# First keys from ScalarE's queue, first queries pooled by VectorE, and new due times in an attention and expert kernel

## The chip, the cores and the metric

The kernel runs on one core of one Trainium2 chip. The metric is the device time of one execution in microseconds. Times of single steps come from one profiled execution, counted from the start of its span.

## What is computed

```python
q_pool = q.reshape(B, H, S // 2, 2, D).mean(axis=3)      # 2, 8, 576, 64
scores = q_pool @ k.T / sqrt(D)                           # 576 x 1152 for each head
attn = softmax(scores);  x = attn @ v                     # heads side by side: 1152 x 512
p = domain_probs / domain_probs.sum(-1)
x = sum over 4 experts: p[:, e] * (relu(x @ w1[e]) @ w2[e])
out = (silu(x @ w_gate) * (x @ w_val)) @ w_out            # 1152 x 512
```

All in float32 to the outside, with S = 1152, D = 64. Inside, operands of most products are split into a high and a low half (`hi`, `lo`) that are multiplied separately.

## The kernel before

The attention is cut into 32 units. A unit is one head and half of its pooled queries (288 of them); 16 units make a batch element. A unit is computed transposed: nine chunks of 128 keys each give a score tile of 128 keys x 288 queries (`score`, two matmuls for each chunk: the query's high and low half). ScalarE copies the scores of two chunks at a time out of PSUM (`copy_scores`, L566), VectorE takes the running maximum over chunks (`max_scores`, acc, L577; L573 and L574 for the ninth). TensorE transposes the maximum (`turn_max`, mt, L583), VectorE reduces it (top, L593), TensorE spreads it over the partitions (m, L605). VectorE and POOL subtract it (L622), ScalarE takes the exponential (L628), TensorE multiplies with the values (av, L655), and ScalarE and VectorE take numerator and denominator (num, den). In the second batch element the exponentials are split as well (eh on ScalarE, el on VectorE or POOL, L640).

Keys and queries come in raw and are turned by TensorE. Keys of two heads are loaded together (`load_k`); a key tile is turned in three groups of three chunks (`prep_k`, L492) into PSUM and split per head: the high half by ScalarE (kt, L508), the low half by VectorE (L510). Queries of two units are loaded together (`load_q`, L475) and pooled: POOL adds each two neighbours and copies the sum beside itself (`prep_pool`, L484 and L485). TensorE turns them (`prep_q`, L518), ScalarE takes the high half (qhi, L529) and VectorE the low one (qlo, L534). The names in the rows of the order are these tiles: kraw and qraw raw keys and queries, tr their transposes in PSUM, kt, qhi and qlo the split operands, s a unit's scores, sc scores in PSUM.

The work of the experts fills TensorE between the units: `experts` multiplies the first batch element's rows with the first weights. Eight hidden tiles of the first expert get the first half of their sum early (part); later the other half follows, VectorE adds the early part (L996), ScalarE takes the high half with the relu (hhi) and VectorE the low half (hlo, L1005).

What order all this stands in is set by `Plan`: each step is given a due time, an engine, a cost and what it reads, writes and takes (buffers, PSUM banks). `Plan.arrange` replays the steps with these costs, each engine taking the ready step of the lowest due time, and the program is written in that order. The due times come from the table `DUE`, one value for each kind of step and phase: units 0 to 7, 8 to 15, 16 to 31. The numbers `E0_START`, `E00_START`, their rates and the `SPLIT` pairs place the experts' products and weight splits. The chip then runs each engine's row strictly in order.

At the start everything is due at once: SP's queue issues two query transfers, six key transfers (three groups, two heads), then the values. The first three key groups and the two query transposes use the PSUM banks c and d.

Of the kernel before, what the change touches and what calls it, by code (L numbers as in the profile page):

```python
# [8 lines left out]
F32 = mybir.dt.float32  # L9
# [20 lines left out]
    "mt": (4.55, -10.52, 4.08),  # L30
    "top": (15.12, 6.72, 2.47),
    "mb": (0, 7.53, 0.71),
    "mcopy": (4.54, 5.02, 2.02),
    "sub0": (5.37, 5.37, 6.98),
    "sub1": (10.75, 19.17, 24.25),
    "sub2": (18.85, 13.58, 25.88),
    "exp0": (25.25, 26.41, 12.68),
    "exp1": (26.62, 16.94, 14.5),
    "exp2": (15.82, 20.58, 17.57),
    "hi0": (14.41, 14.41, 24.01),  # L40
    "hi1": (16.21, 16.21, 16.21),
    "hi2": (16.25, 16.25, 16.25),
    "lo0": (13.1, 13.1, 13.1),
    "lo1": (15, 15, 15),
    "lo2": (17.1, 17.1, 17.1),
    "av": (18.94, 17.93, 11.82),
    "finish": (-54.35, -171.81, -27.68),
    "inv0": (0.7, 0.7, 0.7),
    "inv1": (2.54, 2.54, 2.54),
    "scale": (2.4, 2.4, 2.4),  # L50
    "xhi": (3.2, 3.2, 3.2),
    "xlo": (3.7, 3.7, 3.7),
    "copy": (-0.74, -7.74, -2.17),
    "max": (0.25, 0.25, -12.78),
    "q0": (-9.93, 3.24, 2.94),
    "q1": (3.52, 4.53, -1.14),
    "qhalf": (0.4, -0.01, -3.27),
    "k0": (-7.53, -3.37, -11.67),
    "k1": (-1.07, 0.04, -2.03),
    "k2": (6.33, 3.09, 6.04),  # L60
    "v": (6.7, 6.7, 9.56),
    "khalf": (-0.27, -0.27, -0.27),
}
SPLIT = (0.43, 4.71)
EARLY_SPLIT = (4.47, 10.35)
E0_START = 162.2
E0_RATE = 9.292
E00_START = 95.52
E00_RATE = 1.625
# [164 lines left out]
def tile_kernel(  # L234
# [14 lines left out]
    P = 128  # L249
# [168 lines left out]
    def load_k(jj, n=KC):  # L418
        b, j = divmod(jj, NPAIR)
        kr = raw.tile([P, KC, 2, D], F32, tag="kraw", name=f"kraw{jj}")  # L420
        for c in range(0, KC, n):
            for i in range(2):
                src = k[b, 2 * j + i].rearrange("(p c) d -> p c d", c=KC)
                nc.sync.dma_start(out=kr[:, c : c + n, i, :], in_=src[:, c : c + n])
        kraws[jj] = kr
# [54 lines left out]
    def prep_pool(g):  # L480
        qr = qps[g] = qraws.pop(g)
        rows = qr.rearrange("p a b d -> p (a b) d")
        first, second = rows[:, :, 0:D], rows[:, :, D : 2 * D]
        nc.gpsimd.tensor_tensor(out=first, in0=first, in1=second, op=ALU.add)  # L484
        nc.gpsimd.tensor_copy(out=second, in_=first)  # L485
# [209 lines left out]
    def plan_attention():  # L695
        def during(u):
            phase = 2 if u >= UPB else u // (UPB // 2)
            return {name: times[phase] for name, times in DUE.items()}
# [6 lines left out]
        def due_k(jj, g, t, bank):  # L705
# [4 lines left out]
            for i in range(2):  # L710
                at(
# [25 lines left out]
        def due_load_k(jj, t, n=KC):  # L737
            parts = [("kr", jj, g) for g in range(3)]
            at(t, "SP", 1.0, load_k, jj, n, writes=parts, takes=[("kraw", ("kraw", jj))])

        def due_load_q(g, t):
            tag = "acc" if g == 1 else "qraw"
            at(t, "SP", 0.9, load_q, g, writes=[("qr", g)], takes=[(tag, ("qr", g))])
# [4 lines left out]
        def due_pool_q(g, t):  # L748
            at(t, "POOL", 1.5, prep_pool, g, writes=[("qr", g)], kind="port")

        start = -20
        due_load_q(0, start)
        due_load_k(0, start, 3)
# [7 lines left out]
        due_k(0, 0, start, "d")  # L761
        due_k(0, 1, start + 1, "d")
        due_k(0, 2, start + 1, "c")
        due_q(1, start + 2, "d")
# [1153 lines left out]
```

## Time and profile before

| | us |
|---|---|
| median of 3 runs | 884.59 (883.41 to 884.64) |
| profiled execution, its own time | 884.53 |
| span of the profiled execution | 882.8 |
| TensorE (PE) busy | 860.8 |
| VectorE (DVE) busy | 648.8 |
| ScalarE (ACT) busy | 518.5 |
| POOL busy | 449.7 |

The span runs from the first to the last instruction; 1.7 us lie around it. A busy time counts an engine's instructions with the tail of each, so a busy TensorE may still start its matmuls further apart than it could. What an engine waits for is read from its rows: the number in brackets behind an instruction is the idle time before it and the step that ended it.

### The profile page before, as it was taken

What the parts mean: (1) busy time and instruction counts of PE and PEld (TensorE: products, weight loads), DVE (VectorE), ACT (ScalarE), POOL (GpSimd) and SP (SyncE); (2) the same over time, 40 slices, a digit from 0 to 9 for tenths busy, and PEclk for the clock granted to TensorE, in tenths of its full rate; (3) what the DMA queues carried; (4) which work ended last, traced back from release to release, by engine and by line L of the source; (5) the groups of instructions that cost most, each with busy time, mean ns of one, the idle gap of its engine ahead of it and who ended that gap; (6) DMA issues with size and microseconds to landing.
All of it is one profiled execution on the core that took longest, in us unless ns stands there. A gap on an engine that the chain in (4) does not pass through costs nothing.

```text
span 882.8 us, 14130 instructions
## 1 busy us (share of the span) xinstructions
PE 860.8 (98%) x5292; PEld 789.4 (89%) x5292; DVE 648.8 (73%) x956; ACT 518.5 (59%) x887; POOL 449.7 (51%) x326
## 2 busy tenths in 40 slices
PE   5999999989999999999999999999999999999998
PEld 4788888778888889888899999999999999998886
DVE  5788888897667777656587778987659977886550
ACT  5888888886787777767343342343335455555422
POOL 3666764976777987978423324533011444336000
PEclk9999999999999999999999999999999999999999
DMA  6112232132323322221357788887451122221202
GB/s 147 42 41 76 55 90 62 56 96 79 101 63 87 98 68 69 61 72 48 109 172 246 249 246 255 268 267 226 147 167 36 43 86 83 94 92 34 99 25 108
DMA packets 131317, 98.48 MB, mean 112 GB/s; under 512 B 33328, under 2 KB 118320, under 8 KB 131248
## 3 DMA queue, kind: packets, MB, share of 16 engines
q1 hardware_dynamic: 131248, 97.57, 36.7%
q8 instruction: 42, 0.69, 0.3%
q14 instruction: 27, 0.22, 0.1%
HBM read 82.07 MB, written 15.48 MB: 111 GB/s over the span
## 4 chain that ended last, share of the span: by engine, by line
PE 90%; DVE 4%; ACT 4%; issue 1%; DMA 0%; POOL 0%; SPq 0%; DVEq 0%; ACTq 0%; POOLq 0%
PE ps L938 45%; PE P L938 14%; PE av L655 12%; PE out L938 8%; PE sc L548 4%; PE sc L549 4%; ACT s L566 1%; PE mt L583 1%; ACT s L628 1%; DVE acc L577 1%; PE m L605 1%; PE tr L492 1%; PE tr L518 1%; DVE kt L510 0%; ACT kt L508 0%
## 5 line engine op out<-in xcount | busy, mean ns | idle before, releaser
L372 ACT ACTIVATE whi<-wraw 128x512 fp32r<-128x512 f32 x128 | 80.7, 630 | 136.5 <-PE ps L938 111.9
L622 POOL TENSOR_TENSOR s<-s,m 128x864 f32<-128x864 f32 x64 | 134.0, 2112 | 47.0 <-ACT m L615 46.1
L938 PE MATMUL ps<-xhi,whi 128*128 128x320 f32 (+1 forms) x384 | 131.4, 342 | 1.0 <-DVE hlo L1005 0.9
L938 PE MATMUL ps<-hhi,whi 128*128 128x320 f32 (+1 forms) x384 | 130.4, 339 | 0.2 <-DVE hlo L1005 0.2
L938 PE MATMUL ps<-hhi,wlo 128*128 128x320 f32 (+1 forms) x384 | 129.3, 337 | 0.1
L938 PE MATMUL ps<-xhi,wlo 128*128 128x320 f32 (+1 forms) x384 | 129.3, 337 | 0.0
L938 PE MATMUL ps<-xlo,whi 128*128 128x320 f32 (+1 forms) x384 | 129.2, 336 | 0.0
L938 PE MATMUL ps<-hlo,whi 128*128 128x320 f32 (+1 forms) x384 | 129.2, 336 | 0.0
L378 DVE TENSOR_TENSOR wlo<-wraw,whi 128x512 fp32r<-128x512 f32 x96 | 84.9, 884 | 40.9 <-ACT whi L372 39.8
L566 ACT ACTIVATE s<-sc 128x576 f32<-128x576 f32 (+1 forms) x160 | 93.5, 599 | 20.8 <-PE sc L549 18.9
L628 ACT ACTIVATE s<-s 128x864 f32<-128x864 f32 x96 | 87.9, 922 | 15.5 <-DVE s L622 12.4
L548 PE MATMUL sc<-qhi,kt 128*128 128x288 f32 x288 | 93.2, 340 | 3.8 <-DVE acc L577 3.6
L549 PE MATMUL sc<-qlo,kt 128*128 128x288 f32 x288 | 81.4, 298 | 0.0
L938 PE MATMUL P<-opT,wq 128*128 128x288 f32 x576 | 81.0, 296 | 0.4 <-ACT s L1388 0.3
L938 PEld LDWEIGHTS P<-opT,wq 128*128 128x128 f32 x576 | 78.1, 188 | 0.9 <-ACT s L1388 0.6
L655 PE MATMUL av<-s,v 128*128 128x288 f32 x288 | 78.6, 411 | 0.0
L938 PEld LDWEIGHTS ps<-hhi,wlo 128*128 128x128 f32 x384 | 72.1, 188 | 5.7 <-DVE wlo L378 0.4
L938 PEld LDWEIGHTS ps<-xhi,wlo 128*128 128x128 f32 x384 | 72.1, 188 | 5.5
L938 PEld LDWEIGHTS ps<-xhi,whi 128*128 128x128 f32 x384 | 72.1, 188 | 4.8 <-DVE hlo L1005 1.7
L1042 POOL TENSOR_TENSOR yacc<-yacc,yt 128x512 f32<-128x512 f32 (+2 forms) x32 | 39.4, 1243 | 71.9 <-DVE yt L1021 66.5
L938 PEld LDWEIGHTS ps<-hhi,whi 128*128 128x128 f32 x384 | 72.1, 188 | 4.3 <-DVE hlo L1005 0.5
L938 PEld LDWEIGHTS ps<-hlo,whi 128*128 128x128 f32 x384 | 72.1, 188 | 3.9
(120 smaller groups left out, 2014.1 us busy)
## 6 DMA issues: line engine op xcount, KB each, us to landing
wraw<-in_moe_w_dram SPq DMA_DIRECT2D x128, 256.0 KB, 2.9
w<-in_moe_w_gate_dram SPq DMA_DIRECT2D x12, 512.0 KB, 5.1
w<-in_moe_w_val_dram SPq DMA_DIRECT2D x12, 512.0 KB, 5.1
wd<-wk SPq DMA_DIRECT2D x12, 512.0 KB, 3.1
w<-in_moe_w_out_dram SPq DMA_DIRECT2D x12, 512.0 KB, 4.3
wr<-wd SPq DMA_DIRECT2D x12, 512.0 KB, 4.1
qraw<-in_q_dram SPq DMA_DIRECT2D x32, 144.0 KB, 2.5
wd<-ws SPq DMA_DIRECT2D x12, 384.0 KB, 4.9
```

Source lines behind the costliest of these rows:

```text
L372: nc.scalar.activation(out=hi, in_=t, func=AF.Copy)
L378: eng.tensor_tensor(out=lo, in0=t, in1=hi.bitcast(F32), op=ALU.subtract)
L492: nc.tensor.matmul(pt[:, m * P : (m + 1) * P], kr[:, c].rearrange("p h d -> p (h d)"), ident, is_transpose=True,)
L518: nc.tensor.matmul(pt[:, t * QT : (t + 1) * QT], qp[:, i, t, :], ident[:QT, :QT], is_transpose=True,)
L548: nc.tensor.matmul(ps, wt, qhi, start=True, stop=False)
L549: nc.tensor.matmul(ps, wt, qlo, start=False, stop=True)
L566: nc.scalar.activation(out=s[:, c : c + n, :], in_=ps[:, :n, :W], func=AF.Copy)
L622: eng.tensor_tensor(out=sg, in0=sg, in1=m.unsqueeze(1).to_broadcast([P, 3, W]), op=ALU.subtract)
L628: nc.scalar.activation(out=sg, in_=sg, func=AF.Exp)
L655: nc.tensor.matmul(avs[u][:, :W], w[:, c].rearrange("p t d -> p (t d)"), e, start=(c == 0 and n == 0), stop=(c == KC - 1 and n == len(term ...
L938: nc.tensor.matmul(ps, w, x, start=first and n == 0, stop=last and n == len(terms) - 1)
L1042: eng.tensor_tensor(out=y, in0=y, in1=t, op=ALU.add)
```

## The change

Four things. (1) `load_k` can load a part of a key tile, and the parts ahead of the last go out from ScalarE's queue: the first head pair's first two key groups are issued by ScalarE, ahead of its table load, and the third by SP behind the queries. (2) `prep_pool` of the first query tile runs on VectorE, the others stay on POOL. (3) The first keys' transposes use banks e, f and d, and each group's split of the second head gets a due time of its own (`START_I0` to `START_I2`); the groups and the second query get due times of their own as well. (4) Units 0 to 2 are a phase of their own with a fourth column in `DUE`, and some 25 values of the other columns and of the experts' placement are changed. No step is added or dropped otherwise.

```diff
 DUE = {
-    "top": (15.12, 6.72, 2.47),
+    "top": (6.99, 6.72, 2.47, 9.2),
-    "sub1": (10.75, 19.17, 24.25),
+    "sub1": (7.26, 19.17, 23.94, 10),
...
-E0_START = 162.2
-E0_RATE = 9.292
-E00_START = 95.52
-E00_RATE = 1.625
+E0_START = 163.36
+E0_RATE = 9.454
+E00_START = 93.4
+E00_RATE = 1.465
+START_I0 = 4.6
+START_I1 = 6.6
+START_I2 = 8.6
+START_K1 = 0.5
+START_K2 = 1.0
+START_Q1 = -0.04
...
-    def load_k(jj, n=KC):
+    def load_k(jj, n=KC, first=0, last=KC):
         b, j = divmod(jj, NPAIR)
-        kr = raw.tile([P, KC, 2, D], F32, tag="kraw", name=f"kraw{jj}")
-        for c in range(0, KC, n):
+        if jj not in kraws:
+            kraws[jj] = raw.tile([P, KC, 2, D], F32, tag="kraw", name=f"kraw{jj}")
+        kr = kraws[jj]
+        eng = nc.sync if first or last == KC else nc.scalar
+        for c in range(first, last, n):
             for i in range(2):
                 src = k[b, 2 * j + i].rearrange("(p c) d -> p c d", c=KC)
-                nc.sync.dma_start(out=kr[:, c : c + n, i, :], in_=src[:, c : c + n])
-        kraws[jj] = kr
+                eng.dma_start(out=kr[:, c : c + n, i, :], in_=src[:, c : c + n])
...
-        nc.gpsimd.tensor_tensor(out=first, in0=first, in1=second, op=ALU.add)
-        nc.gpsimd.tensor_copy(out=second, in_=first)
+        eng = nc.gpsimd if g else nc.vector
+        eng.tensor_tensor(out=first, in0=first, in1=second, op=ALU.add)
+        eng.tensor_copy(out=second, in_=first)
...
-            phase = 2 if u >= UPB else u // (UPB // 2)
+            phase = 3 if u < 3 else 2 if u >= UPB else u // (UPB // 2)
...
-        def due_k(jj, g, t, bank):
+        def due_k(jj, g, t, bank, second=None):
...
             for i in range(2):
+                if i and second is not None:
+                    t = second
...
+        at(start, "SP", 0.0, load_k, 0, 3, 0, 6, writes=[("kr", 0, 0), ("kr", 0, 1)],
+           takes=[("kraw", ("kraw", 0))])
         due_load_q(0, start)
-        due_load_k(0, start, 3)
+        at(start, "SP", 1.0, load_k, 0, 3, 6, KC, writes=[("kr", 0, 2)], uses=[("kraw", 0)])
...
-        due_k(0, 0, start, "d")
-        due_k(0, 1, start + 1, "d")
-        due_k(0, 2, start + 1, "c")
-        due_q(1, start + 2, "d")
+        due_k(0, 0, start, "e", START_I0)
+        due_k(0, 1, start + START_K1, "f", START_I1)
+        due_k(0, 2, start + START_K2, "d", START_I2)
+        due_q(1, START_Q1, "c")
```

The line numbers of the changed kernel are higher by 9 in this part (L492 becomes L501, and so on). TensorE's row at the start of the program, before and then after, up to the first score:

```order
L492 MATMUL tr<-ident,kraw_109 128x128 x3
L518 MATMUL tr<-ident,qraw_102 128x96 x3
L492 MATMUL tr<-ident,kraw_109 128x128 x6
L548 MATMUL sc<-qhi_139,kt_128 128x288
L549 MATMUL sc<-qlo_142,kt_128 128x288
```

```order
L501 MATMUL tr<-ident,kraw_102 128x128 x6
L527 MATMUL tr<-ident,qraw_107 128x96 x3
L501 MATMUL tr<-ident,kraw_102 128x128 x3
L527 MATMUL tr<-ident,qraw_107 128x96 x3
L557 MATMUL sc<-qhi_148,kt_129 128x288
L558 MATMUL sc<-qlo_155,kt_129 128x288
```

The second key group has moved ahead of the first query, and the second query, which stood behind four score chunks, now stands ahead of all. ScalarE's row at the same place, before and after (the two kt numbers are the two heads):

```order
L508 ACT_TABLE_LOAD
L508 ACTIVATE kt_128<-tr 64x384
L508 ACTIVATE kt_136<-tr 64x384
L529 ACTIVATE qhi_139<-tr 128x288
L508 ACTIVATE kt_128<-tr 64x384
L508 ACTIVATE kt_136<-tr 64x384
```

```order
L433 DMA kraw_102<-in_k_dram 128x3x64 x4
L517 ACT_TABLE_LOAD
L517 ACTIVATE kt_129<-tr 64x384
L517 ACTIVATE kt_134<-tr 64x384
L517 ACTIVATE kt_129<-tr 64x384
L517 ACTIVATE kt_134<-tr 64x384
L538 ACTIVATE qhi_148<-tr 128x288
```

Four key issues stand ahead of the table load, and four splits of keys instead of two ahead of the query's. TensorE's row around the transpose of unit 4's maximum (mt), before and after; the numbers behind s, qhi and acc are units:

```order
L548 MATMUL sc_546<-qhi4_343,kt2_208 128x288
L549 MATMUL sc_546<-qlo4_347,kt2_208 128x288
L518 MATMUL tr_549<-ident_90,qraw3_438 128x96 x3
L548 MATMUL sc_554<-qhi5_409,kt3_211 128x288
L549 MATMUL sc_554<-qlo5_418,kt3_211 128x288
L548 MATMUL sc_554<-qhi5_409,kt3_211 128x288
L549 MATMUL sc_554<-qlo5_418,kt3_211 128x288
L583 MATMUL mt_570<-ident_90,acc4_490 96x128 x3
```

```order
L557 MATMUL sc_532<-qhi4_342,kt2_208 128x288
L558 MATMUL sc_532<-qlo4_346,kt2_208 128x288
L527 MATMUL tr_541<-ident_90,qraw3_450 128x96 x3
L557 MATMUL sc_552<-qhi5_434,kt3_211 128x288
L558 MATMUL sc_552<-qlo5_438,kt3_211 128x288
L557 MATMUL sc_552<-qhi5_434,kt3_211 128x288
L558 MATMUL sc_552<-qlo5_438,kt3_211 128x288
L664 MATMUL av_561<-s3_387,v1_112 128x288 x3
L592 MATMUL mt_570<-ident_90,acc4_493 96x128 x3
```

The first product of unit 3 with its values, which stood behind the transpose, now stands ahead of it. VectorE's row behind the maximum of unit 16, before and after:

```order
L574 TENSOR_TENSOR acc_1758<-sc,acc_1758 128x288
L640 TENSOR_TENSOR el_0_1808<-s_1635,eh_0_1798 128x864
L534 SCALAR_TENSOR_TENSOR qlo_1815<-tr,qhi_1805 128x288
L672 TENSOR_SCALAR den_1736<-av 64x288
L679 RECIPROCAL den_1736<-den_1736 128x144
```

```order
L583 TENSOR_TENSOR acc_1740<-sc,acc_1740 128x288
L681 TENSOR_SCALAR den_1709<-av 64x288
L543 SCALAR_TENSOR_TENSOR qlo_1806<-tr,qhi_1796 128x288
L688 RECIPROCAL den_1709<-den_1709 128x144
L649 TENSOR_TENSOR el_0_1831<-s_1612,eh_0_1802 128x864
```

The query's low half and a denominator have moved ahead of the subtraction el.

## Rows read from the trace of the kernel before

**Rows 1.** Busy us by stretch: PE, PEld, DVE, ACT, POOL (x instructions), PEclk, DMA share, GB/s.

```profile
176.00:220.00 44.00, 41.47 (x231) 35.35 (x230) 37.26 (x54) 34.39 (x58) 31.59 (x21) 1.00 0.30 84
...
240.00:400.00 160.00, 160.00 (x939) 141.96 (x938) 111.85 (x156) 118.16 (x196) 132.59 (x79) 1.00 0.26 73
```

**Rows 2.** PE's waits, 0 to 45 us: us in total, times, longest.

```profile
PE sc L548 <- DVE acc L577: 3.6, 4, 1.1
```

**Rows 3.** Instructions in order of time, opening: start, us, engine, line, operation, [idle before].

```profile
0.73 1.28 ACT L508 ACT_TABLE_LOAD   x1 [0.73 <-PEq L1898]
...
3.94 0.99 POOL L484 TENSOR_TENSOR qraw<-qraw 96x384 f32<-96x384 f32 x1 [0.61 <-DMA qraw<-in_q_dram]
...
4.99 0.50 POOL L485 COPY qraw<-qraw 96x384 f32<-96x384 f32 x1
...
5.07 0.87 PE L492 MATMUL tr<-ident,kraw 128*128 128x128 f32 x3 [5.07 <-POOL qraw L484]
...
5.98 0.98 ACT L508 ACTIVATE kt<-tr 64x384 fp32r<-64x384 f32 x2 [3.97 <-PE tr L492]
...
6.99 1.12 DVE L510 TENSOR_TENSOR kt<-tr,kt 64x384 fp32r<-64x384 f32 x2 [6.99 <-ACT kt L508]
...
8.15 0.46 DVE L534 SCALAR_TENSOR_TENSOR qlo<-tr,qhi 128x288 fp32r<-128x288 f32 x1
...
9.38 0.59 PE L548 MATMUL sc<-qhi,kt 128*128 128x288 f32 x1
...
11.14 0.65 ACT L566 ACTIVATE s<-sc 128x576 f32<-128x576 f32 x1
...
11.21 0.44 PE L549 MATMUL sc<-qlo,kt 128*128 128x288 f32 x1
...
13.15 0.76 DVE L577 TENSOR_TENSOR acc<-sc,s 128x576 f32<-128x576 f32 x1
```

**Rows 4.** The second key issue, its size and landing time; DMA share by stretch.

```profile
2.19 0.49 SPq L424 DMA_DIRECT2D kraw<-in_k_dram  x1
kraw<-in_k_dram SPq DMA_DIRECT2D x1, 96.0 KB, 2.7
2.00:4.00 2.00, 0.00 (x0) 1.00 0.84 219
```

**Rows 5.** Instructions around the second unit's maximum; PE's clock at 24 us.

```profile
23.86 0.61 PE L548 MATMUL sc<-qhi,kt 128*128 128x288 f32 x1 [1.09 <-DVE acc L577]
...
24.99 2.73 PE L655 MATMUL av<-s,v 128*128 128x288 f32 x6
...
25.49 0.46 DVE L574 TENSOR_TENSOR acc<-sc,acc 128x288 f32<-128x288 f32 x1
...
27.55 0.49 PE L583 MATMUL mt<-ident,acc 128*96 128x128 f32 x3
24.00:26.00 2.00, 2.00 (x7) 0.50 0.00 0
```

**Rows 6.** PE's waits at maxima, 0 to 220 us; unit 4's maximum and its neighbours.

```profile
PE mt L583 <- DVE acc L574: 1.6, 3, 0.8
...
PE mt L583 <- ACT num L674: 0.4, 1, 0.4
49.21 0.93 ACT L628 ACTIVATE s<-s 128x864 f32<-128x864 f32 x1 [0.61 <-DVE s L622]
...
51.57 0.50 PE L583 MATMUL mt<-ident,acc 128*96 128x128 f32 x3 [0.50 <-DVE acc L574]
```

**Rows 7.** DVE and PE where the second batch element begins.

```profile
166.77 1.47 DVE L640 TENSOR_TENSOR el<-s,eh 128x864 fp32r<-128x864 f32 x1
168.66 0.47 PE L518 MATMUL tr<-ident,qraw 96*128 96x96 f32 x3 [1.15 <-DVE qlo L534]
176.97 0.69 DVE L996 TENSOR_TENSOR ps<-ps,part 128x512 f32<-128x512 f32 x1
184.35 0.68 DVE L1005 SCALAR_TENSOR_TENSOR hlo<-ps,hhi 128x512 fp32r<-128x512 f32 x1
```

More of the change, by code (lines that the diff above doesn't have):

```diff
@@ L29 @@
 DUE = {
-    "mt": (4.55, -10.52, 4.08),
-    "top": (15.12, 6.72, 2.47),
-    "mb": (0, 7.53, 0.71),
-    "mcopy": (4.54, 5.02, 2.02),
-    "sub0": (5.37, 5.37, 6.98),
-    "sub1": (10.75, 19.17, 24.25),
[L36 to L60, printed above, removed]
@@ L61 @@
-    "v": (6.7, 6.7, 9.56),
-    "khalf": (-0.27, -0.27, -0.27),
-}
-SPLIT = (0.43, 4.71)
-EARLY_SPLIT = (4.47, 10.35)
-E0_START = 162.2
-E0_RATE = 9.292
-E00_START = 95.52
-E00_RATE = 1.625
+    "mt": (4.55, -10.52, 4.08, 9),
+    "top": (6.99, 6.72, 2.47, 9.2),
+    "mb": (0, 7.53, 0.71, 15.04),
+    "mcopy": (4.54, 5.02, 2.02, 9.6),
+    "sub0": (5.37, 5.37, 6.98, 9.8),
+    "sub1": (7.26, 19.17, 23.94, 10),
+    "sub2": (18.85, 13.58, 23.73, 10.2),
+    "exp0": (26.3, 20.44, 12.68, 26.6),
+    "exp1": (26.62, 26.29, 14.5, 19.93),
@@ new lines @@
+    "exp2": (15.82, 20.58, 17.57, 20.72),
+    "hi0": (14.41, 14.41, 23.17, 14.41),
+    "hi1": (16.21, 16.21, 16.21, 16.21),
+    "hi2": (16.25, 16.25, 16.25, 16.25),
+    "lo0": (13.1, 13.1, 13.1, 13.1),
+    "lo1": (15, 15, 15, 15),
+    "lo2": (17.1, 17.1, 17.1, 17.1),
+    "av": (18.94, 17.93, 11.82, 14),
+    "finish": (-95.32, -171.81, -41.97, -23.08),
+    "inv0": (0.7, 0.7, 0.7, 0.5),
+    "inv1": (2.54, 2.54, 2.54, 0.6),
+    "scale": (2.4, 2.4, 2.4, 1),
+    "xhi": (3.2, 3.2, 3.2, 66.33),
@@ new lines @@
+    "xlo": (3.7, 3.7, 3.7, 2.2),
+    "copy": (-0.74, -7.74, -2.17, 0.1),
+    "max": (-1.22, 0.25, -12.78, 0.05),
+    "q0": (-9.93, 6.56, 1.52, 4),
+    "q1": (5.93, 4.53, -1.14, 8),
+    "qhalf": (-25.93, -0.01, -3.27, 0.2),
+    "k0": (-7.53, -3.37, -11.67, -16.41),
+    "k1": (-3.17, -8.79, 4.67, -22.99),
+    "k2": (2.71, 6.76, 4.38, 8),
+    "v": (6.7, 6.7, 16.25, 6.7),
+    "khalf": (-0.27, -0.27, -0.27, -45.09),
+}
+SPLIT = (0.43, 3.35)
+EARLY_SPLIT = (-1.79, 8.61)
+E0_START = 163.36
+E0_RATE = 9.454
@@ L748, in due_pool_q @@
         def due_pool_q(g, t):
-            at(t, "POOL", 1.5, prep_pool, g, writes=[("qr", g)], kind="port")
+            at(
+                t, "POOL" if g else "DVE", 1.5 if g else 0.8, prep_pool, g,
+                writes=[("qr", g)], kind="port",
+            )
         start = -20
+        at(start, "SP", 0.0, load_k, 0, 3, 0, 6, writes=[("kr", 0, 0), ("kr", 0, 1)],
+           takes=[("kraw", ("kraw", 0))])
         due_load_q(0, start)
-        due_load_k(0, start, 3)
+        at(start, "SP", 1.0, load_k, 0, 3, 6, KC, writes=[("kr", 0, 2)], uses=[("kraw", 0)])
         due_pool_q(0, start)
```

## The prediction, made before the changed kernel was run

> **What bounds the kernel now.** I read the busy time by stretch first [rows 1]. From 240 to 400 us TensorE is busy for 160.00 of 160.00 us: nothing it does there can start earlier. From 176 to 220 it is busy for 41.47 of 44. So the change can only win in the opening and in the short waits of the first 220 us, and what it wins there stays won, because the stage behind is TensorE's own. In the opening TensorE first idles until its first transpose at 5.07 us [rows 3], and then, by the list of waits [rows 2], four times, 3.6 us together, for the running maximum that VectorE takes out of PSUM (acc). The row at 5.07 names POOL's pooling as what ended its wait. The code says otherwise: `prep_k` needs the keys and the identity alone. The second key issue starts at 2.19 us and lands 2.7 us later, at 4.89 [rows 4]; the transpose starts at 5.07 [rows 3]. The pooling merely ended at the same time.
>
> The sum is made against the profiled execution: 884.53 us, of which 882.8 is the span and 1.7 lies around it. The median of the runs is 884.59, so the two are one number here. About 0.2%, 1.8 us, is what a measurement of this kernel can tell from no change: faster means under 882.8, slower over 886.4.
>
> **The opening, step by step.** *Keys.* ScalarE issues the first four key transfers from 0.73 us on, where its table load starts now [rows 3]; the load (1.28 us) moves behind four issues of 0.5, to 2.75 to 4.03, and is hidden, since its first split came at 5.98 before. The DMA engines are the limit: from 2 to 4 us they are 84% busy at 219 GB/s [rows 4], so at most 260 GB/s is to be had. Before, 480 KB (two query issues of 144 KB, two of keys) landed with the second key issue, 2.24 us at 219 GB/s. Now about 384 KB do (two key issues and as much on SP's queue), 1.51 us at 260: 0.73 earlier, at 4.16, and the first transpose at 4.3 instead of 5.07. If the keys travelled as if alone it would be 4.1; if the second queue gave nothing, 4.6.
>
> The Trainium skill (DMA: Bandwidth & Descriptors, section Issuing engines are not separate DMA queues) says that transfers from several engines run on the same 16 DMA engines and interleave, so that a second issuing engine saves issue time alone. The 84% agrees. By that rule the opening's term below would be about nothing, the sum 882.4, and the case is the second rival.
>
> *Queries.* They now share the engines with the keys. The second query transfer landed in time for the pooling at 3.94; now 576 KB must be through, 2.27 us at 260, so it lands at about 4.9. On VectorE the add of 96x384 lies between 0.46 (128x288, [rows 5]) and 0.69 (128x512, [rows 7]), I take 0.55; the copy is not shown, at most the same 0.46 and at least half of it, I take 0.35. On POOL they took 0.99 and 0.50 [rows 3]. The pooling ends near 6.1, after 5.49 before: cheaper arithmetic, later data. VectorE has nothing else until 6.2, so nobody queues behind it.
>
> *Splits.* TensorE's row of work is now: two key groups, a query, the third group, the other query, and then the scores. The second head's keys are not split later on ScalarE: its row still has both heads of a group one behind the other, and now four splits (0.98 a pair [rows 3]) instead of two stand ahead of the query's. Pair one runs 5.25 to 6.2; the second group's keys land near 5.7 (768 KB), its transposes end at 6.5, and pair two runs 6.75 to 7.7; the query's high half, taken at the low half's 0.46 or less, ends at 8.2. On VectorE one low half of the keys (0.56, half of the pair's 1.12 [rows 3]) precedes the query's low half, which ends at 8.8 against 8.61 before [rows 3]. The second query's transposes wait for it (same bank), take some 0.5 and end at 9.4, so the first score starts at 9.4, where it started at 9.38. What is won lies behind that: these transposes and ScalarE's last splits no longer stand between the scores. Eight score matmuls, 0.26 us apart as from 9.38 to 11.21 before [rows 3], end at 11.5, their copies (0.65) at 12.2, and the first maximum runs at 12.25 instead of 13.15: 0.9 us.
>
> *Given back.* Behind it VectorE is the chain. The next head's second key group is now split before the first unit's maximum is reduced, 2 x 0.56 us that stood behind it. That delays the reduce and everything it releases, so the third unit's first scores come at 23.9 to 24.2, against 23.86 [rows 5]; the second unit's maximum, which no longer has those splits ahead, ends some 0.4 us before its 25.95. What the next step of TensorE, the transpose of that maximum (27.55), makes of it hangs on the clock: from 24 to 26 the granted clock is 0.50, the lower level of 1.2 GHz, after a stretch with many waits [rows 5]. If that comes again, the transposes stand at 27.3 to 27.8; if not, at 26.2. The opening gives between -0.2 and +1.3 us; I take **0.5**, nearer the low end, since the work of the stretch before the fall is the same.
>
> **Later rows.** *Maxima.* TensorE waited at the transposes of maxima for VectorE's last step: 1.6 us in three waits, the longest 0.8, and 0.4 put down to ScalarE [rows 6]. In the new row the product with the values of unit 3 stands ahead of the maximum of unit 4, and likewise for unit 5; at unit 8 two more score chunks do. Its exponential ended at 50.14 [rows 6], before TensorE would reach it, so its six matmuls, 2.73 us at the lower clock [rows 5] and some half of that at the upper one, fill the 0.50 of idle time. The longest wait, unit 7's, is not covered. At stake is 1.6 - 0.8 + 0.4 = 1.2; the maxima then come later by up to 0.9, which the next reduce must absorb. I take **1.0**, bounds 0 and 1.2.
>
> *A query behind a subtraction.* At 168.66 TensorE idles 1.15 for a query's low half that stands behind the 1.47 us subtraction (el) on VectorE [rows 7]. In the new row the query's half stands ahead of it, and expert products stand between the two transposes. I take **1.15**, bounds 0 and 1.15.
>
> *The rest* of the moved due times (expert start, later units) I cost at nothing: TensorE covers them from 220 us on, where it never waits. Before that, bounds of -1.3 (half the 2.53 us idle from 176 to 220 [rows 1]) and +2.7 (the last rival). The sum: 884.53 - 0.5 - 1.0 - 1.15 = **881.9**.
>
> **Rivals.** *Nothing is left.* VectorE is busy for 37.26 of 44 us from 176 to 220 [rows 1], and in the opening it is the chain. Then a wait that is filled with work pulled ahead comes back where that work is missing, and the opening returns its 0.9 at the third unit. 884.3, within 883 to 886. For it: the first score does not move. Against it: from 220 on TensorE has work in hand.
>
> *Two queues, one rate.* If both queues together move no more than the 219 GB/s of before, the second key group lands at 6.2 instead of 5.7 and every later step of the opening is 0.6 late: first score at 10.0, lead at the first maximum 0.3, and at the third unit a loss of some 0.4 that the lower clock does not return. 884.53 + 0.4 - 1.0 - 1.15 = 882.8. For it: the engines are at 84%. Against it: from 84 to 100% there is room.
>
> *All terms at their ends.* 1.3 + 1.2 + 1.15 + 1.3 = 4.9: 879.6. It needs the clock to stay at 2.4 GHz from 24 to 26 and VectorE's crowd near 180 to thin out.
>
> *Slower.* Between the maxima of units 17 and 18 the new row of TensorE has six expert products where it had two. Two products take one addition of the early part and one low half on VectorE, 0.69 + 0.68 us [rows 7], so four more cost it 2.74 in front of the next maximum and subtraction. If VectorE has no gap there, TensorE waits that long: 884.53 + 2.74 - 0.5 = 886.8. It decides as soon as VectorE stands idle for less than 2.7 us between those maxima. Against it: the same products leave the crowd behind them.
>
> **Numbers.** Forecast 881.9, chance 0.37 (0.34 of it under 882.8). One rate 0.10 (0.06 faster, 0.04 the same). Nothing left 0.28 (0.26 the same, 0.02 faster). All ends 0.12, faster. Slower 0.13, of which 0.11 over 886.4. That gives faster 0.54, same 0.35, slower 0.11. The range, 879.6 to 886.0, leaves out half of the ends case and nearly all of the slower one.
>
> **What would show it.** First transpose near 4.3, pooling on VectorE ending near 6.1, first score near 9.4, first maximum near 12.3, second unit's maximum transposed before 27.5. No idle time before the maxima of units 4, 5 and 8; no wait of 1 us before a query's transposes near 165. I am wrong in the opening if the first score comes at 8.5 or earlier (then keys or queries landed sooner than 260 GB/s allows), or if TensorE waits again beyond 220 us.

## The result, and the profile after

The changed kernel takes 893.1 us (892.74 to 893.43, four runs), the kernel before 884.0 (883.07 to 884.64): a ratio of 1.0104, 95% interval 1.0086 to 1.0121. It is slower by 1%, where 881.9 was forecast. The page of the profiled execution shows the same instructions on every engine as before, but for two that went from POOL to VectorE. VectorE is busy 11.2 us longer, of which the two are 0.9; for the rest the same instructions take longer.

```profile
span 891.0 us, 14119 instructions
...
PE 865.3 (97%) x5292; PEld 790.6 (89%) x5292; DVE 660.0 (74%) x958; ACT 517.2 (58%) x887; POOL 444.3 (50%) x324
```

The two stretches that answer to [rows 1], with the same columns: from 240 to 400 us TensorE is still without a gap, and from 176 to 220 it has lost 1.8 us of busy time.

```profile
176.00:220.00 44.00, 39.66 (x228) 33.86 (x229) 37.24 (x52) 35.28 (x62) 35.73 (x24) 1.00 0.31 87
240.00:400.00 160.00, 160.00 (x933) 141.80 (x932) 115.61 (x157) 117.97 (x199) 129.65 (x81) 1.00 0.27 78
```

TensorE's waits over the whole span (us in total, times, longest) answer to [rows 2, 6]. The waits at maxima (mt) have shrunk to 0.2 us. Before they were 2.5: the 2.0 of [rows 6], and one of 0.5 for a split of keys that [rows 6] leaves out. Those of the scores for acc went from 3.6 to 2.5. In their place stand waits that the kernel before has not, or has smaller:

```profile
PE tr L501 <- DMA kraw<-in_k_dram: 7.2, 3, 4.9
PE ps L954 <- DVE hlo L1021: 2.8, 3, 1.5
PE sc L557 <- DVE acc L586: 2.5, 5, 1.1
PE sc L557 <- ACT s L575: 1.8, 2, 1.0
PE tr L527 <- DVE qlo L543: 1.4, 2, 1.0
PE tr L527 <- DVE kt L519: 1.4, 2, 0.7
PE ps L954 <- DVE yt L1037: 0.9, 1, 0.9
...
PE mt L592 <- ACT s L637: 0.2, 1, 0.2
```

The opening, in order of time, answers to [rows 3]. The first transpose starts 0.2 us earlier, not 0.8; the second key group 1.2 us later than forecast; the first score, at 10.43, a full 1.05 later than before.

```profile
4.61 0.56 DVE L493 TENSOR_TENSOR qraw<-qraw 96x384 f32<-96x384 f32 x1 [4.61 <-DMA qraw<-in_q_dram]
...
4.86 0.87 PE L501 MATMUL tr<-ident,kraw 128*128 128x128 f32 x3 [4.86 <-DMA kraw<-in_k_dram]
5.20 0.36 DVE L494 COPY qraw<-qraw 96x384 f32<-96x384 f32 x1
...
6.96 0.88 PE L501 MATMUL tr<-ident,kraw 128*128 128x128 f32 x3 [1.22 <-DMA kraw<-in_k_dram]
...
10.43 0.59 PE L557 MATMUL sc<-qhi,kt 128*128 128x288 f32 x1
...
13.41 0.76 DVE L586 TENSOR_TENSOR acc<-sc,s 128x576 f32<-128x576 f32 x1 [1.27 <-ACT s L575]
```

**Where the time went.** Both kernels run the same matmuls, in another order. So I measure lateness at equal work: each matmul counts for the lower quartile of the start-to-start distances of its kind in the kernel before (0.131 us for a score matmul, 0.227 for a product of 512 columns); the sum so far is the work done, and a start's time less that sum is its lateness. The table gives each kernel's lateness less that of the kernel before, in its profiled execution, at six points; the head says when the kernel before is there.

| kernel | 28 us | 116 | 181 | 194 | 236 | 492 |
|---|---|---|---|---|---|---|
| changed | +1.4 | +4.2 | +5.5 | +7.5 | +7.1 | +8.2 |
| e1 open only | +1.7 | +3.7 | +5.1 | +4.4 | +4.1 | +5.3 |
| e2 due only | +0.5 | +5.3 | +7.0 | +7.8 | +7.3 | +16.8 |
| e3 keys one queue | +1.4 | +4.3 | +5.0 | +7.0 | +6.6 | +7.7 |
| e4 values behind keys | +3.7 | +6.8 | +7.8 | +7.9 | +7.5 | +9.6 |
| e5 bank order | +0.8 | +3.6 | +4.5 | +6.6 | +6.1 | +6.1 |
| e6 experts old | +0.5 | +3.2 | +15.5 | +15.4 | +16.6 | +40.2 |
| e7 column 0 old | +1.7 | +3.0 | +10.6 | +11.3 | +15.3 | +18.2 |
| e8 columns 1, 2 old | +1.9 | +5.8 | +9.3 | +9.1 | +8.9 | +25.0 |
| e9 key buffer | +2.4 | +5.2 | +5.5 | +7.6 | +7.2 | +8.3 |
| e10 split behind | +1.8 | +5.0 | +6.0 | +5.6 | +13.2 | +14.6 |
| e11 quick open | 0.0 | 0.0 | 0.0 | 0.0 | 0.0 | 0.0 |
| e12 POOL pools | -0.5 | +2.4 | +3.3 | +5.3 | +4.8 | +6.0 |
| e13 query ahead | -1.1 | -1.1 | -1.1 | -1.1 | -1.1 | -1.1 |
| e14 maxima covered | +0.8 | +1.8 | +1.8 | +1.8 | +1.8 | +1.9 |
| e15 el first | +0.6 | +0.5 | +0.6 | -0.3 | -0.3 | -0.3 |
| e16 three moves | +0.5 | +1.4 | +1.6 | +0.8 | +0.9 | +0.9 |
| e17 values cover | +1.6 | +8.8 | +8.8 | +8.8 | +8.8 | +8.8 |
| e18 before banks | -0.9 | -0.9 | -0.8 | -0.8 | -0.8 | +0.3 |

The changed kernel's 8.2 us are thus: 1.4 in the opening, 2.8 from 28 to 116 us, 1.1 at a key transfer behind that, 2.0 in the crowd on VectorE from 181 to 194, 1.1 at one wait near 450, and -0.2 for the rest. The first column varies between executions of one and the same row: e13 to e18 start with the row of the kernel before and lie between -1.1 and +1.6. What a move is worth is therefore the change along its line of the table.

### The profile page after: what moved, and what is told of

It reads as the page before. It is cut to its first block, busy times and chain, and to the rows that moved or that the text cites. A ratio compares the mean times of both kernels' runs of the same rounds, so it can differ in the third digit from the quotient of the medians.

```text
span 891.0 us, 14119 instructions
## 1 busy us (share of the span) xinstructions
PE 865.3 (97%) x5292; PEld 790.6 (89%) x5292; DVE 660.0 (74%) x958; ACT 517.2 (58%) x887; POOL 444.3 (50%) x324
## 4 chain that ended last, share of the span: by engine, by line
PE 89%; DVE 4%; ACT 4%; DMA 1%; issue 1%; ACTq 0%; SPq 0%; DVEq 0%
PE ps L954 44%; PE P L954 14%; PE av L664 12%; PE out L954 8%; PE sc L557 4%; PE sc L558 4%; ACT s L575 1%; DMA kraw<-in_k_dram 1%; PE mt L592 1%; DVE acc L586 1%; ACT s L637 1%; PE m L614 1%; PE tr L527 1%; PE tr L501 1%; DVE kt L519 1%
## 5 line engine op out<-in xcount | busy, mean ns | idle before, releaser
L631 POOL TENSOR_TENSOR s<-s,m 128x864 f32<-128x864 f32 x64 | 131.7, 2077 | 61.4 <-ACT m L624 61.4
L384 DVE TENSOR_TENSOR wlo<-wraw,whi 128x512 fp32r<-128x512 f32 x96 | 92.0, 959 | 48.0 <-ACT whi L378 39.1
L649 POOL TENSOR_TENSOR el<-s,eh 128x864 fp32r<-128x864 f32 x32 | 68.3, 2142 | 22.7 <-ACT eh L642 22.6
```

What stands on the lines that cost most here:

```text
L384: eng.tensor_tensor(out=lo, in0=t, in1=hi.bitcast(F32), op=ALU.subtract)
L631: eng.tensor_tensor(out=sg, in0=sg, in1=m.unsqueeze(1).to_broadcast([P, 3, W]), op=ALU.subtract)
L649: eng.tensor_tensor(out=lo, in0=src, in1=parts[u, g][0].bitcast(F32), op=ALU.subtract)
```

## The experiments

**Halves of the change.** In e1 only the opening, in e2 only the later values are new:

```diff
 e1, from the changed kernel:
-    "top": (6.99, 6.72, 2.47, 9.2),
+    "top": (15.12, 6.72, 2.47, 9.2),
...
 e2, from the kernel before:
-    "top": (15.12, 6.72, 2.47),
+    "top": (6.99, 6.72, 2.47, 15.12),
...
```

> The changed kernel's opening (keys from ScalarE's queue, first query pooled on VectorE, banks e, f, d, the fourth column for units 0 to 2), with the first three columns of DUE, E0_START, E00_START, their rates and both SPLIT pairs as before. Behind matmul 1067 its row on TensorE is the one of before. Theory A (the later due times cost most): the trace of the changed kernel is 1.4 us late at 10 us of TensorE work and 7 to 8 late at the end, so this kernel should be 1.4 us slower than before: 885.5 (884.8 to 886.5). Theory B (the opening's lateness grows on its way through the later units): 889 to 893.

> The reverse: the opening and units 0 to 2 as before, the first three columns of DUE, the experts' starts and rates and the SPLIT pairs as in the changed kernel. Theory A: 8.2 - 1.4 = 6.8 us slower than before: 891 (889.5 to 892.5). Theory B: 884 to 886. The two kernels add up to the change (+9 us together) if the parts don't work on each other.

Measured: e1 889.1 (ratio 1.0045, 1.0029 to 1.0060), e2 901.7 (1.0184, 1.0162 to 1.0205). Neither theory holds for both: e1 lies where theory B had it, e2 9 us and more above both. The parts cost 0.45% and 1.84%, the whole 1.04%: they are not a sum.

**Groups of values.** Each of three kernels has one group of the later values as before, all else as in the changed kernel:

```diff
 e6:
-E0_START = 163.36
+E0_START = 162.2
...
 e7:
-    "top": (6.99, 6.72, 2.47, 9.2),
+    "top": (15.12, 6.72, 2.47, 9.2),
...
 e8:
-    "sub1": (7.26, 19.17, 23.94, 10),
+    "sub1": (7.26, 19.17, 24.25, 10),
...
```

> The changed kernel with E0_START, E0_RATE, E00_START, E00_RATE, SPLIT and EARLY_SPLIT as before. Theory V (each wait belongs to the values that moved its steps): TensorE's waits for the low half of the hidden tiles (hlo, 2.8 us in three between 184 and 198 us, 1.1 before) go back to about 1, so 891; the waits from 30 to 125 us stay. Theory W (any row that the plan makes from a mixture is some us worse than one that was kept, whichever value differs): 889 to 900, with waits at new places.

> The changed kernel with the first column of DUE (units 3 to 7) as before. Theory V: the lateness that it gathers from 40 to 95 us (2.8 us in waits for key splits, for copies on ScalarE and for a PSUM bank) goes, the rest stays: 890.3. Theory W: 889 to 900, with waits at new places.

> The changed kernel with the second and third column of DUE (units 8 to 31) as before. Theory V: the wait for keys at 121.8 us (1.3) and about half of the 2.0 us lost from 182 to 198 us go: 891. Theory W: 889 to 900, with waits at new places.

Measured: 923.9 (1.0429), 903.4 (1.0198), 911.6 (1.0289). Theory W, and worse than it said. In the stretch where its values act, e7 does gain (from 28 to 116 us it loses 1.3 us where the changed kernel loses 2.8), but it then loses 7.6 from 116 to 181, where nothing of its own was undone. In e6 and e7 TensorE waits 4.6 and 4.1 us in one piece for a denominator (den), a wait that neither parent has. A due time decides which of the ready steps comes first, so each value shifts all that follows; a value can't be priced apart from the others. A part of the loss is TensorE's clock: in the profiles of e2, e6, e7 and e8 it falls to 1.2 GHz once or twice more (e6: granted clock 0.50 from 194.8 to 201.6 us and from 293.8 to 300.6), which it doesn't in the kernel before and in the changed one between 40 us and the end. Why just these rows are so bad was not followed further.

**The opening.** e3 sends all keys from SP's queue behind the queries again, e4 takes the first values off SP's queue, e12 pools on POOL, and e11 is the kernel before with the first key group ahead of the queries and VectorE pooling:

```diff
 e3:
-        eng = nc.sync if first or last == KC else nc.scalar
+        eng = nc.sync
...
 e4:
+        if first:
+            for i in range(2):
+                nc.scalar.dma_start(out=vts[i][:, :, i, :], in_=values(0, i))
...
 e12:
-        eng = nc.gpsimd if g else nc.vector
+        eng = nc.gpsimd
 e11, from the kernel before, in load_q:
+        if g == 0:
+            load_k(0, 3)       
...
+        eng = nc.gpsimd if g else nc.vector
```

> The changed kernel with one difference: the first four key transfers go out from SP's queue behind the two queries, as before; the rows of the compute engines are unchanged. Theory Q (the second queue makes the second key group late: it landed at 6.9 us, since SP's queue sent queries, third group and values at the same time): second group near 5.7, first score near 9.3 instead of 10.43, first maximum's transpose near 18.8 instead of 19.80, time 892.1 (1 us less than the change). Theory R (the new row of TensorE is late by itself: two key groups and both queries ahead of the scores): first score 10.0 to 10.4 and 893 again.

> The changed kernel with the first two value transfers taken off SP's queue and issued from ScalarE's, behind the four keys and ahead of the table load. Theory Q1 (the values passed the keys): the second group lands at 5.7 to 6.2, first score 9.3 to 9.8. Theory Q2 (whatever stands on SP's queue takes its share, and now that is the second query): the second group stays at 6.7 to 7.0, first score 10.3 to 10.5, no difference in time to the change. Theory R: no difference either.

> The changed kernel with the first query pooled on POOL again (0.99 and 0.50 us instead of 0.56 and 0.36 on VectorE), rows otherwise unchanged. Theory K (the opening waits for the second key group, which lands at 6.9): the query's transposes stay at 7.6 us, nothing changes. Theory L (the query is the bound): first score 0.6 us later.

> The kernel before with two edits in the opening and its rows otherwise unchanged: the first key group of both heads goes out ahead of the queries on SP's queue, and the first query is pooled on VectorE. First transpose near 3.9 instead of 5.07, first score near 8.4 instead of 9.38. Theory C: 1 us less than before. Theory D: the lead is gone by the third unit (the changed kernel with all keys on one queue reached the first score 0.8 us earlier than with two and had none of it left at 28 us): less than 0.3 us.

Measured: e3 890.8 (1.0056), e4 893.4 (1.0091), e12 891.2 (1.0065), e11 885.2 against 885.8 (0.9994, 0.9981 to 1.0007). In e3 the second group's transposes start at 6.13 instead of 6.96 and the first score at 9.66 instead of 10.43, so theory Q holds for the start, by 0.8 us of the 1.1 that it said; but at 28 us e3 is as late as the changed kernel. In e11 the first score comes at 8.63, 0.75 earlier than before, and at 28 us the lead is 0.05 us. In e4 the second group came at 7.19 us: Q2. In e12 the query's transposes stand at 7.54 and the first score at 10.34, theory K. In these single profiles no edit of the first 10 us shows a gain at 28 us that is clear of the spread given below. The runs leave more open: e3 and e12 took 2.3 and 1.9 us less than the changed kernel (four runs each), so the second queue and the pooling on VectorE may each have a part in its loss. That was not settled.

Why the keys were late shows in the DMA queues of the changed kernel from 2.1 us to 5.95, when the last packet of its keys has gone (packets, MB, share of 16 engines; q10 is ScalarE's queue, and the keys of the first two groups are all that it carries):

```profile
DMA packets 3246, 0.92 MB, mean 239 GB/s; under 512 B 2774, under 2 KB 3246, under 8 KB 3246
## 3 DMA queue, kind: packets, MB, share of 16 engines
q1 hardware_dynamic: 1646, 0.53, 61.3%
q10 hardware_dynamic: 1600, 0.39, 52.1%
```

Both queues send about as many packets, but SP's are larger in part, and so it moves more bytes: the keys that TensorE waits for share the way with the queries, the third group and the first values. In e4 it is the same, 1523 and 1618 packets from 2.1 to 6.05 us. The last key transfer, issued at 2.3, lands 4.5 us later, at 6.8, and the transposes start at 6.96. On one queue (e3) what is due later stands behind the keys.

What moves the first column from one execution to the next is for the most part TensorE's clock. From 24 to 28 us (busy us, instructions, granted clock) the kernel before is partly at 1.2 GHz:

```profile
24.00:28.00 4.00, 4.00 (x14) 0.60 0.01 4
```

and e13, with the same row up to there and as little work from 20 to 24 us (1.96 busy us against 1.95), stays at 2.4 GHz:

```profile
24.00:28.00 4.00, 3.81 (x23) 1.00 0.02 4
```

At the start, too, the score matmuls stand 0.24 us apart, against 0.13 later, up to 12.7 us in the kernel before, up to 18.0 in the changed one, and up to 21.9 in e9 with the changed one's row, though the granted clock reads 1.00 there. The runs say the same: of the 76 executions of the kernel before that stand beside the experiments, the 20 with a mean granted clock of 1.00 took 884.3 us on average, the 14 with 0.994 took 886.1, the 2 with 0.990 888.4. The mean of the first column is +0.25 for the eight kernels that start with the old row (the kernel before, e2, e13 to e18) and +1.5 for the eight with the new (the changed kernel, e1, e5 to e10): the opening costs some 1.3 us on average. This is an estimate, from single executions that lie 2.7 us apart with the old row and 1.9 with the new.

**The place of the banks.** e5 hands out the PSUM banks of the changed kernel in the old order, e18 those of the kernel before in the new one:

```diff
 e5, behind single(); e18 the same with e, f, c, d, p0, p2:
+    for tag in ("d", "c", "p0", "p2", "f", "e"):
+        (pair if tag[0] == "p" else single)(tag, "place")
```

> The changed kernel with the PSUM banks handed out in the order of the kernel before (d, c, p0, p2, f, e instead of e, f, c, d, p0, p2); every engine's row is unchanged. In the changed kernel TensorE idles 0.94 us at 451.7 us, at the first expert product of the second batch element, until VectorE's yt has read the last sum of the first; before, and with the later due times alone, it doesn't. Theory P (the place of the banks does it: the new opening takes e and f first, so the second PSUM pool lies on other banks): that wait goes, 1.2 us less than the change, 891.9. Theory N (VectorE is late there for another reason): the wait stays and the time is 893.

> The kernel before with its PSUM banks handed out in the order of the changed one (e, f, c, d, p0, p2), every engine's row unchanged. Theory P: the first expert product of the second batch element waits 0.9 us for yt, near 444 us, and 1.2 us are lost at the end. Theory N: no wait, no difference.

Measured: e5 890.7 (1.0053, 1.0034 to 1.0072); e18 886.5 against 885.5 (1.0011, 1.0001 to 1.0020). Theory P. The wait of the changed kernel,

```profile
451.68 0.38 PE L954 MATMUL ps<-xhi,whi 128*128 128x320 f32 x1 [0.94 <-DVE yt L1037]
```

is gone in e5, and e18 has it with no other change:

```profile
443.78 0.38 PE L941 MATMUL ps<-xhi,whi 128*128 128x320 f32 x1 [0.95 <-DVE yt L1024]
```

The wait costs e18 1.1 us from 236 to 492 us in the table, as it costs the changed kernel, and e5 nothing. The reason, by the code: the second PSUM pool lies where the first one's tags lay in the order in which they were first asked for, and now the first bank that it needs is the one whose last sum VectorE reads last. The trace doesn't name banks, but fits: in e5 the product starts at 449.62, ahead of the same yt at 449.89.

**The key transfer.** e9 loads the fifth pair's keys into a buffer that is free:

```diff
-            kraws[jj] = raw.tile([P, KC, 2, D], F32, tag="kraw", name=f"kraw{jj}")
+            pool, tag = (acc, "acc") if jj == 4 else (raw, "kraw")
+            kraws[jj] = pool.tile([P, KC, 2, D], F32, tag=tag, name=f"kraw{jj}")
```

> The changed kernel with the keys of the fifth head pair loaded into a buffer that stands free at that time; every engine's row is unchanged. In the changed kernel that load is issued at 117.7 us, when the old keys' last transposes let go of the buffer, and lands at 123.1: TensorE idles 1.1 us and VectorE 2.0 behind it. Here it is issued some 2 us earlier and both waits go. Theory C (what TensorE or VectorE lose before 180 us stays lost): 1.1 us at the end, up to 2.0 if VectorE's idle time counts. Theory D (the crowd on VectorE from 188 to 212 us takes such differences up): TensorE is 1.1 us earlier at 130 us and less than 0.4 at 220.

Measured: 892.7 (1.0073, 1.0049 to 1.0097). In the changed kernel the transfer and its first users stand so:

```profile
117.66 1.32 SPq L433 DMA_DIRECT2D kraw<-in_k_dram  x2
...
123.15 0.52 PE L501 MATMUL tr<-ident,kraw 128*128 128x128 f32 x3 [1.11 <-DMA kraw<-in_k_dram]
```

In e9 the issue comes at 116.68, 1.0 us earlier and not 2, and the wait is gone. The changed kernel goes from +4.2 to +5.3 at this point (126 us), e9 from +5.2 to +5.4, and the difference stays to the end: theory C. That the two profiled executions hardly differ (892.8 and 892.7) is the opening, 1.0 us later in e9's.

**The crowd on VectorE.** e10 moves one step in the changed kernel, e15 one in the kernel before:

```diff
 VectorE's row in e10:
-wlo<-wraw,whi 128x512
 hlo<-ps,hhi 128x512
 el<-s,eh 128x864
 qlo<-tr,qhi 128x288
+wlo<-wraw,whi 128x512
 VectorE's row in e15:
+el<-s,eh 128x864
 ps<-ps,part 128x512
-el<-s,eh 128x864
```

> The changed kernel with one step of VectorE moved: the low half of the ninth weight tile (wlo, 2.54 us at 195.3), which with the SPLIT pair of the changed kernel stands ahead of a hidden tile's low half (hlo), the subtraction el and a query's low half, stands behind these three. TensorE waited for the first and the last of these for 1.5 and 1.0 us at 198.5 and 201.0. Theory D (VectorE's row sets the pace from 188 to 201 us): both waits go or shrink and 1.5 to 2.5 us are won at the end. Theory S (VectorE is full until 212 us, so the wait only moves): less than 0.5 us, with a new wait between 201 and 212.

> The kernel before with one step of VectorE moved: the el of unit 17, 2.77 us at 187.84 while POOL runs its own el from 187.62 (1.19 where it runs alone), ahead of the addition of 0.69 at 187.24. Theory P (whichever of the two engines starts first holds the other up): VectorE's el takes 1.2 us from 187.3, POOL's starts or ends later, TensorE's wait of 1.22 at 190.66 goes and about 1.2 us are won. Theory N (el takes long for another reason): 2.8 us again, nothing won.

Measured: e10 895.1 (1.0115, 1.0086 to 1.0145); e15 884.1 against 885.0 (0.9990, 0.9978 to 1.0001). In the changed kernel wlo takes 2.54 us beside two subtractions on POOL:

```profile
195.21 4.50 POOL L649 TENSOR_TENSOR el<-s,eh 128x864 fp32r<-128x864 f32 x2
195.26 2.54 DVE L384 TENSOR_TENSOR wlo<-wraw,whi 128x512 fp32r<-128x512 f32 x1
...
198.46 0.50 PE L954 MATMUL ps<-xhi,whi 128*128 128x512 f32 x1 [1.49 <-DVE hlo L1021]
```

e10 won what theory D said, 2.4 us against the changed kernel from 181 to 194 us, and lost 7.6 from there to 236, when its steps met POOL's again:

```profile
207.35 1.22 POOL L499 COPY qraw<-qraw 96x384 f32<-96x384 f32 x1
208.12 5.01 DVE L389 TENSOR_TENSOR wlo<-wraw,whi 128x512 fp32r<-128x512 f32 x1
208.53 4.05 POOL L654 TENSOR_TENSOR el<-s,eh 128x864 fp32r<-128x864 f32 x2
```

The step of 0.67 us ends at 213.13, 0.55 after POOL's pair. Not all of the 7.6 is this: TensorE waits 1.6, 1.2 and 1.7 us from 203 to 216, and the granted clock is 0.50 from 215.2 to 222.0 us. This execution took 899.2 us, the three others 894.3 to 895.7 with a mean clock of 0.996 and 0.997 in place of 0.992, so most runs of e10 lose less. In the kernel before POOL is the first at unit 17:

```profile
187.62 2.08 POOL L640 TENSOR_TENSOR el<-s,eh 128x864 fp32r<-128x864 f32 x1
187.84 2.77 DVE L640 TENSOR_TENSOR el<-s,eh 128x864 fp32r<-128x864 f32 x1
```

In e15 VectorE is first:

```profile
187.80 1.34 DVE L647 TENSOR_TENSOR el<-s,eh 128x864 fp32r<-128x864 f32 x1
188.15 2.89 POOL L647 TENSOR_TENSOR el<-s,eh 128x864 fp32r<-128x864 f32 x1
```

el takes 1.34 us instead of 2.77, POOL's 2.89 instead of 2.08, and the line of the table falls by 0.9 us and stays there: theory P, with 0.9 in place of 1.2 (the interval of its time just includes no gain). The Trainium skill (SBUF — State Buffer, section SBUF: two separate sides) calls the port pair that the two engines share an exclusive lock: of POOL and a VectorE step with two inputs in SBUF, who starts first has it for the whole instruction and the other stands still. These rows agree: 2.77 and 2.08 with POOL first, 1.34 and 2.89 with VectorE first.

**The forecast's own moves, alone.** In the kernel before, e13 puts one query's low half ahead of el, e14 two score chunks ahead of four maxima, e17 the product with the values ahead of the same four, and e16 joins e13, e14 and e15:

```diff
 VectorE's row in e13:
+qlo<-tr,qhi 128x288
 el<-s,eh 128x864
-qlo<-tr,qhi 128x288
 TensorE's row in e14, at units 4, 5, 7 and 8:
-mt<-ident,acc 96x128 x3
 sc<-qhi,kt 128x288
...
+mt<-ident,acc 96x128 x3
 TensorE's row in e17, at the same units:
+av<-s,v 128x288 x3
 mt<-ident,acc 96x128 x3
...
-av<-s,v 128x288 x3
```

> The kernel before with one step of VectorE moved: the low half of the query of unit 18 ahead of the subtraction el of unit 16 instead of behind it, the one reorder that the forecast paid 1.15 us for. Theory C (a wait taken away ahead of the crowd stays taken away): TensorE's wait of 1.15 us at 168.66 goes and 1.1 us are won at the end. Theory D (the crowd on VectorE decides, since el is now 0.45 us later and nothing is taken off VectorE): TensorE is early at 172 us and less than 0.3 us ahead at 220.

> The kernel before with the transposes of the maxima of units 4, 5, 7 and 8 (waits of 0.50, 0.39, 0.77 and 0.37 us, 2.0 together) each put behind the next two score chunks. Theory C: 1.5 to 2.0 us are won. Theory E (the reduce behind each maximum comes 0.2 to 0.5 us later, and what it releases with it, so that the wait comes back at the next score chunk or sum): less than 0.5 us, or a loss.

> The three moves together in the kernel before. Theory C: 1.1 + 1.8 + 1.2 = 4 us less than before, 880. Theory D: between before and 1.2 us less, since only what relieves VectorE near 190 us counts.

> The kernel before with the first product with the values of units 3, 4, 6 and 7 put ahead of the transposes of the maxima of units 4, 5, 7 and 8, as the forecast had it for units 4 and 5. Theory C: the waits of 2.0 us are filled, 1.5 to 2.0 won. Theory F (the product needs the bank that the unit before it still holds: VectorE takes the denominator out of it behind the same maximum, at 51.45 to 51.91 us for unit 4): TensorE waits longer than before, 0.3 to 0.5 us for each of the four, and 1 to 2 us are lost.

Measured: e13 885.3 against 885.0 (1.0001, 0.9989 to 1.0012), e14 886.1 (1.0010, 0.9997 to 1.0022), e16 885.0 (0.9999, 0.9988 to 1.0011), e17 893.1 against 885.5 (1.0087, 1.0067 to 1.0106). In e13 the transposes no longer wait (they stand at 166.43), and the next score does:

```profile
169.92 0.40 PE L555 MATMUL sc<-qhi,kt 128*128 128x288 f32 x1 [0.98 <-ACT s L573]
```

In e14 the list of waits from 30 to 110 us reads as in [rows 6], with sc in place of mt:

```profile
PE sc L555 <- DVE acc L581: 1.6, 3, 0.8
PE sc L555 <- ACT num L681: 0.5, 1, 0.5
```

The filling chunk itself waited for the bank that the same maximum lets go. Theory E; 1.0 us is lost from 28 to 116 us of the profiled execution, while the interval of the time does not exclude zero. In e17, at unit 4:

```profile
52.59 0.46 DVE L581 TENSOR_TENSOR acc<-sc,acc 128x288 f32<-128x288 f32 x1
...
53.07 0.46 DVE L679 TENSOR_SCALAR den<-av 64x288 f32<-64x288 f32 x1
...
53.68 1.69 PE L662 MATMUL av<-s,v 128*128 128x288 f32 x6 [1.00 <-DVE den L679]
55.21 0.49 PE L590 MATMUL mt<-ident,acc 128*96 128x128 f32 x3
...
55.74 0.55 DVE L600 TENSOR_REDUCE top<-mt 96x3 f32<-96x384 f32 x1 [1.72 <-PE mt L590]
...
57.76 0.40 PE L555 MATMUL sc<-qhi,kt 128*128 128x288 f32 x1 [1.00 <-DVE acc L584]
```

The product needs the bank out of which den is taken, behind the same maximum, so TensorE waits 1.00 instead of 0.50; VectorE then waits 1.72 for the late transpose, and TensorE a second time for VectorE. Theory F by its cause and about four times dearer: 7.2 us from 28 to 116 us, 1.8 on average at each of the four places. e16 is the sum of its parts: -0.8 for el, +0.9 for the maxima, 0 for the query.

e17 prices the filling with VectorE's row of before. In the changed kernel VectorE's row is another: there den stands ahead of the last step of the maximum, and at unit 4 the product waits for nothing:

```profile
52.63 0.46 DVE L681 TENSOR_SCALAR den<-av 64x288 f32<-64x288 f32 x1
...
53.28 1.62 PE L664 MATMUL av<-s,v 128*128 128x288 f32 x6
...
53.98 0.46 DVE L583 TENSOR_TENSOR acc<-sc,acc 128x288 f32<-128x288 f32 x1
...
54.74 0.49 PE L592 MATMUL mt<-ident,acc 128*96 128x128 f32 x3
```

Still nothing is won. From 30 to 110 us TensorE waited 2.0 us before, all at maxima; in the changed kernel it waits 2.9, at other steps:

```profile
PE sc L557 <- ACT s L575: 0.8, 1, 0.8
PE tr L527 <- DVE kt L519: 0.7, 1, 0.7
PE tr L527 <- PE av L664: 0.6, 1, 0.6
PE tr L501 <- DVE kt L519: 0.4, 1, 0.4
PE sc L557 <- DVE acc L586: 0.2, 1, 0.2
PE mt L592 <- ACT s L637: 0.2, 1, 0.2
```

That is 0.9 of the 2.8 us lost from 28 to 116; the rest stands in no wait of these lists and was not followed.

## Why the prediction was wrong, step by step

**What bounds the kernel: right in part.** TensorE has no gap from 240 to 400 us, and lateness gathered before that is never won back (no line of the table falls by more than 0.1 us from 236 to 492). That TensorE "never waits" from 220 us on holds for the kernel before, where one wait of 0.3 is left, and not for others: e2, e6 and e8 lose 9 to 24 us from 236 to 492, and in the changed kernel the change of banks made one of 0.94 at 451.7, the sign of being wrong that I had named. Rows on all engines were equal there, and I took equal rows for equal times.

**Keys: the term was mis-sized.** I let both queues share 260 GB/s by equal halves and had the second group at 5.7, with 768 KB through. They shared by packets, not by bytes: when the keys' last packet had gone, at 5.94, 0.97 MB were through, 0.39 of them the keys', at 239 GB/s from 2.1 us on; the landing came at 6.8. The rival "two queues, one rate" had 6.2 for it and was nearer. The Trainium skill (DMA: Bandwidth & Descriptors, section Issuing engines are not separate DMA queues), as quoted in the prediction, says that only issue time is saved. The trace agrees that no more was: the first transposes came 0.2 us earlier and the second group's, against one queue, 0.8 later.

**Queries: right.** The add took 0.56 and the copy 0.36, estimated at 0.55 and 0.35; the pooling ended at 5.56, forecast 6.1, since its data came at 4.6 and not 4.9, and nothing waited for it (e12).

**First score 9.4, first maximum 12.3: wrong by a us,** since both hang on the second group: 10.43 and 13.41. What I then said of the third unit held better than its numbers: in the profiles of e3 and e11 a lead at the first score is gone at 28 us. Instead of 0.5 won, the opening costs about 1.3 by the estimate above.

**Maxima, 1.0: the step that failed.** The waits did go in the changed kernel, the four of [rows 6] from 2.0 to 0.2, and I took a filled wait for a won one. From 30 to 110 us 2.7 us of waits at other steps stand in their place. In the kernel before, e14 and e17 price the filling alone at 1.0 and 7.2 us lost. I had seen that the exponential of unit 3 was done when the product would be reached, but not its other inputs: in the old row of VectorE the bank it writes is let go by den, which stands behind the very maximum that TensorE waits for. The new row has den ahead of it at unit 4, and in the whole list of its waits none of av for den is left, so e17's cause is not what cost the changed kernel its time.

**A query behind a subtraction, 1.15: the second step that failed.** e13 does that move alone, the wait goes and 0.98 of it stands at the next score. In the changed kernel, too, TensorE waits 1.0 us for a copy of scores and 0.4 for a query's low half from 160 to 183 us. The bound of 0 was in the text; I took the other end.

**The rest at nothing: the largest part of the miss.** It is +1.1 at the key transfer, +1.1 at the banks, +2.0 in the crowd, and most of the 2.8 from 28 to 116 us. The first three have a run that takes the cause away or adds it alone (e9, e5 and e18, e10); the 2.8 has none. Ahead of 200 us TensorE did not cover these, though I had put them at nothing.

**Rivals.** "Slower" named the waits for hlo behind expert products: they grew from 1.1 to 2.8 us, 1.7 where 2.74 was set, and stand among those that cost the 2.0 in the crowd. Its sum, 886.8, lacked the other four losses. "Nothing is left" had the mechanism (a filled wait comes back where the filler is missing) and not that it can cost more than it was.

## What to carry to other kernels

A wait on the engine that seems to bound is worth its length only if all that the next steps need is there already: follow the inputs and the output buffer of the filler back, and if one of them comes from the step that is waited for, filling gains nothing (e14) or costs a multiple (e17). Where none does, the wait can still come back at another step, as it did in the changed kernel. A table of due times is one object: take a part of it, and the schedule may be worse than both parents (here 902 to 924 us in four of five mixtures, from parents at 884 and 893). Where rows are equal, ask next what has moved place: banks, buffers, and the moment at which two engines meet.

## What the runs showed of the hardware

- One VectorE subtraction of 128x512 took 0.67 us alone and 5.01 beside a copy and two subtractions on POOL (e10). Which of the two engines starts first decides: one step put ahead of a 0.69 us addition took 1.34 us instead of 2.77 (e15).
- The same first 28 us of TensorE's row lay between 1.1 us ahead of the kernel before (e13) and 1.6 behind it (e17), with the clock. From 12 to 28 us, in steps of 4, the granted clock was 1.00 throughout in e13, and 0.87, 0.50, 0.77 and 0.65 in e17. In e13 and e18 the difference then stayed as it was to 236 us.
- Two DMA queues with work at the same time sent about as many packets each, 1646 and 1600 in 3.85 us, and not as many bytes, 0.53 and 0.39 MB.
